# Turning the second half's tokens on VectorE and through DRAM in a fused attention and Mish MLP kernel

## The chip, the cores and the metric

The kernel runs on one core of a Trainium2 chip. The metric is the device time of one execution in microseconds; all times here are in microseconds unless another unit stands beside them. The engines are named as the profile names them: PE is TensorE's matmul, PEld its weight load, DVE is VectorE, ACT is ScalarE, POOL is GpSimd, and SP is SyncE, on which every DMA of this kernel is issued, in order.

## The reference

```python
xn = _layernorm(x)                        # x: 1 x 2048 x 576
qkv = (xn @ wqkv)                         # 32 heads of 18
# each token attends to 8 tokens: itself and those 2, 4, .. 14 before it
logits = einsum("bhsd,bhswd->bhsw", q, kg) * 18 ** -0.5
o = einsum("bhsw,bhswd->bhsd", softmax(masked logits), vg)
h = xn @ w1 + b1                          # 576 -> 4608
act = h * tanh(softplus(h))               # Mish
return x + o @ wo + act @ w2
```

Everything is fp32.

## The kernel before

**Precision and products.** Every matmul operand is held as a high and a low part: the high part is a cast (ScalarE), the low part what the cast lost (a subtraction on VectorE or GpSimd). A product is three matmuls: high by high, high by low, low by high. On top of that the MLP products are arranged as 2 x 2 block products with fewer multiplications, so that sums of blocks are formed first (names S1 to S4 on the activations' side, T1 to T4 on the weights' side) and their results are added up afterwards.

**Halves, blocks, tiles.** The 2048 tokens are worked on in two halves (`hf` 0 and 1) of 8 tiles of 128 tokens. A half has two blocks (`b` 0 and 1) of 4 tiles (`jj`, or `n` from 0 to 7 over both blocks). `XTs[hf, b]` holds the normalised tokens of a block with the features on the partitions, high and low: four groups of 128 features and a remainder of 64. For block 0 the remainder's tile has a copy in its upper half, for block 1 there is a second remainder with the difference of the two blocks (`rems`, made on GpSimd).

**How the second half's tiles come there.** `x_load(n)` loads a tile, `norm1(n)` normalises it on ScalarE and copies the remainder on GpSimd. `ln_transpose` forms the remainder of the block and calls `transpose_split`: TensorE transposes the tile in 128x128 pieces into two PSUM tiles (five pieces for block 0, six for block 1; `ta` and `tb`, or `tt` where they lie in the banks of the MLP's outputs), ScalarE casts the high part from PSUM (line 81) and VectorE subtracts for the low part (lines 82 and 87).

**The plan.** The program's order is one list of slots, `plan`. A slot has TensorE work of its own: q for one projection item (14 matmuls of 432 columns), m for one of the six parts of an MLP-up round (`m1_part`), p for a chunk or an item of the MLP-down product, z and o for others, t for one tile's transposes. `before(i, fn)` puts background work in front of slot i: loads, casts, low parts, sums, and one step of the attention, which runs beside the rest on GpSimd (products) and VectorE (sums, softmax). The slots' indices, and the offsets in the calls of `before`, are written by hand. `pend` holds the Mish work of a slot until the next one, and `soon` what is to come first in the next slot. Each engine runs its instructions in the order of this list.

**The place in the program.** The last MLP-up round of the first half is `quad(0, 17)`, from 500.89 on. Between its parts stand the down chunks of round 16, and the transposes of block 0 of the second half. Then come the last down chunks of the first half, the projections of the second half (from about 533) with block 1's transposes among them, the part called z, and the second half's MLP. In rounds q = 1 to 8 of that the down product runs in items (e, k) that pair two rounds (`p_item`): `u_sum` forms a sum of activations, `u_high` and `u_low` split it into the unit `u` that TensorE uses. The table `ds` says how many slots before its item each of these three stands. Last come the output projections o, whose operands `o_split` prepares.

Of the kernel before, what the change touches and what calls it, by code (L numbers as in the profile page):

```python
# [8 lines left out]
F32 = mybir.dt.float32  # L9
# [30 lines left out]
def block_kernel(ctx: ExitStack, tc: tile.TileContext, x, wq, wo, w1, b1, w2, mask, out):  # L40
# [23 lines left out]
    for k in range(30):  # L64
        nc.tensor.transpose(warm[:, (k % 4) * P:(k % 4 + 1) * P], ident, ident)

    def transpose_split(src, dst, col, extra=None, pair=False):
        n = next(tpn)
        if pair:
            ta, tb = (ps.tile([P, 512], F32, tag="out", bufs=4, name=f"tt{k}_{n}") for k in range(2))  # L70
        else:
            ta = ps.tile([P, 512], F32, tag="h", bufs=4, name=f"ta_{n}")
            tb = ps.tile([P, 512], F32, tag="h", bufs=4, name=f"tb_{n}")
        for k in range(KT):
            nc.tensor.transpose(ta[:, k * P:(k + 1) * P], src[:, k * P:(k + 1) * P], ident)  # L75
# [27 lines left out]
    def x_load(n):  # L103
        xn = sb.tile([P, 5 * P], F32, tag="xn", bufs=XNB, name=f"xn_1_{n}_{next(tpn)}")
        nc.sync.dma_start(xn[:, 0:D], x_tile(1, n))
        xns[1, n] = xn

# [76 lines left out]
    def ln_transpose(hf, b, jj):  # L184
        if jj == 0:
            XTs[hf, b] = sb.tile([P, 9 + b, TB], F32R, tag=f"xt{b}", bufs=1, name=f"xt_{hf}_{b}")
        xn = xns[hf, b * JB + jj]
        if (b, jj) == (0, 0):
            rems[hf] = sb.tile([P, JB, P], F32, tag="tt", bufs=2, name=f"rem_{hf}")
        rem = rems[hf][:, jj, :]  # L190
        if b == 0:
            nc.gpsimd.tensor_copy(rem, xn[:, KT * P:])
        else:
            nc.gpsimd.tensor_tensor(out=rem, in0=rem, in1=xn[:, KT * P:], op=ALU.subtract)
        transpose_split(xn, XTs[hf, b], jj * P, rem if b else None, (hf, b) == (1, 0) and jj < 3)

    def raw_load(src, width, name):
        raw = sb.tile([P, 5 * P], F32, tag="raw", bufs=4, name=f"r{name}")
# [310 lines left out]
    pend, soon = [], []  # L509

    def attention(hf):
        kqs = [load_kq(hf, k) for k in range(PU)]
# [153 lines left out]
    def prod(ph, wt, off, X, hi, lo, first, last):  # L666
        seq = [(off + k, wl, xs + k) for k in range(2) for wl, xs in ((0, hi), (0, lo), (1, hi))]
        for i, (wk, wl, xs) in enumerate(seq):
            nc.tensor.matmul(ph, wt[:, wl, wk * P:(wk + 1) * P], X[:, xs, :],  # L669
                             start=first and i == 0, stop=last and i == len(seq) - 1,  # L670
                             skip_group_check=True)

    def rest(ph, wt, off, X, xs):
        for wl in range(2):
# [365 lines left out]
    def y_store(j):  # L1040
        nc.sync.dma_start(y_d.rearrange("(p j) d -> p j d", j=TJ)[:, j, :], accs[0][j])
# [100 lines left out]
    plan = []  # L1142
    at = {}
    US = {"q": 2.75, "z": 2.5, "p": 3.15, "t": 0.6, "o": 2.6}
    PART = (3.2, 1.4, 1.4, 1.8, 1.8, 1.8)

    def add(tag, *fns, alias=None):
        at[tag] = at[alias] = len(plan)
# [5 lines left out]
    def qi(hf, g, b, jj, alias=None):  # L1154
        add(("q", hf, g, b, jj), lambda: qkv_item(hf, g, b, jj), alias=alias)
# [5 lines left out]
        add(("m", hf, q, part), lambda: m1_part(hf, q, part), alias=alias)  # L1161

    def pr_(hf, q, b, p, alias=None):
        def end():
            if hf == 0 and q == NP - 1:
                for jj in (2 * p, 2 * p + 1):
                    y_store(b * JB + jj)
        add(("p", hf, q, b, p), lambda: ((m2_cols if hf else m2_pair)(hf, q, b, p), end()), alias=alias)

    items = []  # L1170

# [51 lines left out]
            qkv_item(0, 0, 0, n)  # L1223

    def tr(b, jj):
        add(("t", 1, b, jj), lambda: ln_transpose(1, b, jj))

    CHUNKS = ((1, 0), (1, 1), (0, 0), (0, 1))

    def quad(hf, q):  # L1230
        if q == 0:
            for part, ids in ((0, (0,)), (2, (1, 2)), (1, (3, 4)), (3, (5, 6)), (5, (7, 8)), (4, (9,))):
                for p_ in {}.get(part, ()) if hf else ():
                    zi(JB - 1, p_)
                if part == 5 and hf == 0:
                    qi(hf, NQ - 1, 0, JB - 1)
                mi(hf, 0, part)
                for i in ids:
                    at["s", hf, 0, i] = len(plan) - 1
            return  # L1240
# [169 lines left out]
    for g, (e, k, s) in enumerate(items):  # L1410
        lead = items[g - 3][2] if g >= 3 else spot(1, 0, 5) + 2 * g
        before(lead + 1, lambda e=e, k=k: p_fetch(e, k))
        for qq in range(2):
            ds = {(0, 0): (-6, -5, -5), (0, 1): (-2, -1, 0), (1, 0): (0, -4, -2), (1, 1): (0, -2, -2), (2, 0): (0, -3, -2), (2, 1): (0, -3, -2), (3, 0): (-4, -3, -2), (3, 1): (-4, -2, -1), (4, 0): (0, -3, -3), (4, 1): (0, -3, -2), (5, 0): (-1, -3, -3), (5, 1): (0, -3, -2), (6, 0): (-4, -3, -1), (6, 1): (-4, -3, -2)}[k, qq]
            for d, f in zip(ds[1:], (u_high, u_low)):
                before(s + d, lambda f=f, e=e, k=k, qq=qq: f(e, k, qq))
            s2 = items[7 * e + (0 if k == 5 else k)][2] + ds[0]
            before(s2, lambda e=e, k=k, qq=qq: u_sum(e, k, qq))
# [38 lines left out]
        before(i, lambda n=n: x_load(n))  # L1457
        before(i + 5, lambda n=n: stats1(n))
    before(i + 6, var1)
    i = spot(0, NP - 2, 0)  # L1460
    for jj in range(JB):
        before(i + 2 * jj, lambda jj=jj: x_load(jj))
        before(i + 2 * jj + 6, lambda jj=jj: norm1(jj))
        before(at["t", 1, 0, jj] + 2, lambda jj=jj: x_load(JB + jj))
    for jj in range(JB):
        before(at["p", 0, NP - 1, 1, 1] + jj, lambda jj=jj: norm1(JB + jj))
# [4 lines left out]
    before(items[3][2], x_diff)  # L1471


    att = {}
    T = [0.0]
    for p_ in plan:
        T.append(T[-1] + p_[2])
# [17 lines left out]
    for n in range(steps - len(last_steps)):  # L1495
# [4 lines left out]
    early = {0: (8,), 1: (0, 2, 4, 6, 8), 2: (0, 3, 6), 3: (0, 3, 6), 4: (0, 4, 7), 5: (0, 3, 7), 6: (1, 4, 7),  # L1500
             7: (0, 4, 7), 8: (1, 4, 8), 9: (1, 3, 7)}
    for q in range(NP):
        cuts[1] += [spot(1, q, i) for i in early.get(q, (1, 3, 5, 7, 9))]
# [40 lines left out]
    for i, (fns, bg, _) in enumerate(plan):  # L1544
        first, soon[:] = soon[:], []
        held, pend[:] = pend[:], []
        for fn in first + bg + (fns + held if i == at["m", 0, 1, 0] else held + fns):
            fn()

    last = {}  # L1550
    for ins in list(nc.cur_bb.bb.instructions):
# [43 lines left out]
```

## Time and profile before

| | us |
|---|---|
| median of 3 runs | 1114.43 (1114.26 to 1114.8) |
| the profiled execution | 1114.25 |
| its span | 1112.5 |
| TensorE busy | 1101.6 |
| VectorE busy | 849.5 |
| ScalarE busy | 499.5 |
| GpSimd busy | 790.8 |

The span runs from the first instruction to the last. A row of the timeline or of the waits has the start, the length, the engine, the line, the operation, the output and its inputs, the shapes and how many instructions the row joins; in brackets stands how long the engine was idle before it, and what it then waited for. A row of the groups has the busy time, the mean of one in ns, and the idle time before.

### The profile page before, as it was taken

What the parts mean: (1) busy time and instruction counts of PE and PEld (TensorE: products, weight loads), DVE (VectorE), ACT (ScalarE), POOL (GpSimd) and SP (SyncE); (2) the same over time, 40 slices, a digit from 0 to 9 for tenths busy, and PEclk for the clock granted to TensorE, in tenths of its full rate; (3) what the DMA queues carried; (4) which work ended last, traced back from release to release, by engine and by line L of the source; (5) the groups of instructions that cost most, each with busy time, mean ns of one, the idle gap of its engine ahead of it and who ended that gap; (6) DMA issues with size and microseconds to landing.
All of it is one profiled execution on the core that took longest, in us unless ns stands there. A gap on an engine that the chain in (4) does not pass through costs nothing.

```text
span 1112.5 us, 18203 instructions
## 1 busy us (share of the span) xinstructions
PE 1101.6 (99%) x6550; PEld 1015.2 (91%) x6550; DVE 849.5 (76%) x1367; ACT 499.5 (45%) x917; POOL 790.8 (71%) x639
## 2 busy tenths in 40 slices
PE   9999999999999999999999999999999999999998
PEld 8999899999999999999999889989989999999998
DVE  6369788888889888897656577786776677777786
ACT  5544655544454544555333354433433344343353
POOL 2479777766679688785788676666688976867532
PEclk9999999999999999999999999999999999999999
DMA  6899696868777758675597898565664657776574
GB/s 202 283 312 316 225 356 214 285 233 276 258 242 264 268 208 301 249 249 204 190 323 241 245 375 307 211 196 196 220 222 170 209 195 223 244 288 219 171 232 142
DMA packets 178270, 271.60 MB, mean 244 GB/s; under 512 B 53218, under 2 KB 120068, under 8 KB 178180
## 3 DMA queue, kind: packets, MB, share of 16 engines
q1 hardware_dynamic: 178180, 270.44, 71.6%
q8 instruction: 52, 0.85, 0.3%
q14 instruction: 38, 0.31, 0.1%
HBM read 160.39 MB, written 110.00 MB: 243 GB/s over the span
## 4 chain that ended last, share of the span: by engine, by line
PE 87%; POOL 6%; DVE 3%; issue 2%; ACT 1%; DMA 0%; SPq 0%; POOLq 0%; DVEq 0%; ACTq 0%
PE h L669 28%; PE po L767 21%; PE pq L348 9%; PE po L880 9%; PE po L859 6%; PE h L675 5%; PE o L1063 5%; PE z L446 3%; POOL pv L571 2%; POOL accP L868 1%; POOL pr L533 1%; POOL act L721 1%; POOL s L620 1%; DMA acc<-in_x 0%; PE ta L75 0%
## 5 line engine op out<-in xcount | busy, mean ns | idle before, releaser
L767 PEld LDWEIGHTS po<-w,act 128*128 128x128 f32 x1728 | 236.4, 188 | 6.0 <-POOL act L721 0.4
L767 PE MATMUL po<-w,act 128*128 128x288 f32 x1728 | 240.7, 295 | 0.1
L533 POOL TENSOR_TENSOR pr<-q,kv 128x576 f32<-128x576 f32 x128 | 196.9, 1563 | 8.5 <-DMA q<-q_d 5.0
L721 POOL TENSOR_TENSOR act<-c,act 128x512 fp32r<-128x512 f32 x81 | 107.3, 1325 | 128.6 <-ACT act L720 128.6
L571 POOL TENSOR_TENSOR pv<-L,kv 128x576 f32<-128x576 f32 x128 | 177.9, 1484 | 26.1 <-DVE L L564 21.2
L771 DVE TENSOR_TENSOR acc<-po,acc 128x288 f32<-128x288 f32 x288 | 119.4, 448 | 29.9 <-PE po L767 29.0
L348 PE MATMUL pq<-wq,xt 128*128 128x432 f32 x672 | 136.5, 361 | 1.0 <-ACT xt L81 1.0
L880 PEld LDWEIGHTS po<-w,act 128*128 128x128 f32 x960 | 130.9, 188 | 4.6 <-DVE accP L883 1.8
L880 PE MATMUL po<-w,act 128*128 128x288 f32 x960 | 133.5, 295 | 1.0 <-DVE accP L883 1.0
L348 PEld LDWEIGHTS pq<-wq,xt 128*128 128x128 f32 x672 | 125.0, 188 | 8.0 <-ACT xt L81 1.8
L715 ACT ACTIVATE c<-c,b1c 128x512 f32<-128x512 f32 x81 | 58.7, 725 | 140.7 <-DVE c L714 140.4
L669 PE MATMUL h<-xt,t 128*128 128x512 f32 x432 | 110.6, 391 | 0.5 <-DVE rt L714 0.3
L669 PE MATMUL h<-S,t 128*128 128x512 f32 x432 | 110.5, 391 | 0.0
L577 DVE TENSOR_REDUCE og<-pv 128x144 f32<-128x1152 f32 x64 | 86.0, 1345 | 25.7 <-POOL pv L571 25.6
L669 PE MATMUL h<-xt,wa 128*128 128x512 f32 x432 | 104.1, 390 | 0.0
L538 DVE TENSOR_REDUCE L<-pr 128x64 f32<-128x1152 f32 x64 | 85.8, 1341 | 23.8 <-POOL pr L533 23.7
L703 ACT COPY c<-h 128x512 f32<-128x512 f32 x81 | 47.4, 586 | 124.1 <-PE h L675 73.0
L859 PEld LDWEIGHTS po<-pw,u 128*128 128x128 f32 x672 | 92.2, 188 | 5.4 <-DVE u L813 2.1
L859 PE MATMUL po<-pw,u 128*128 128x288 f32 x672 | 94.3, 295 | 2.5 <-DVE u L813 1.6
L669 PEld LDWEIGHTS h<-xt,wa 128*128 128x128 f32 x432 | 80.9, 188 | 17.0
L669 PEld LDWEIGHTS h<-xt,t 128*128 128x128 f32 x432 | 79.0, 188 | 15.7 <-DVE rt L714 0.7
L883 DVE TENSOR_TENSOR accP<-po,accP 128x288 f32<-128x288 f32 x160 | 68.9, 452 | 29.8 <-PE po L880 28.2
(228 smaller groups left out, 1853.8 us busy)
## 6 DMA issues: line engine op xcount, KB each, us to landing
kv<-kv_d SPq DMA_DIRECT2D x64, 396.0 KB, 5.1
kept_t<-t SPq DMA_DIRECT2D x36, 512.0 KB, 4.8
t<-kept_t SPq DMA_DIRECT2D x36, 512.0 KB, 6.7
rw<-in_w SPq DMA_DIRECT2D x36, 320.0 KB, 4.4
kept_wa<-wa SPq DMA_DIRECT2D x18, 640.0 KB, 4.7
kept_w<-w SPq DMA_DIRECT2D x20, 576.0 KB, 4.1
wa<-kept_wa SPq DMA_DIRECT2D x18, 640.0 KB, 5.2
w<-kept_w SPq DMA_DIRECT2D x20, 576.0 KB, 4.1
```

Of the source, the lines that this page charges most:

```text
L348: nc.tensor.matmul(pq[:, 0:432], XT[:, xi, tok], wt[wi][:, hl, 0:432], start=i == 0, stop=i == len(seq) - 1)
L533: nc.gpsimd.tensor_tensor(out=pr[:, x:x + hh], in0=q[:, j0 + x:j0 + x + hh, None, :].to_broadcast([P, hh, W, CU]), in1=win(kt, 0, CU, j0 + ...
L538: nc.vector.tensor_reduce(L[:, k, j0:j0 + hj].rearrange("p j w h -> p (j w h)"), pr.rearrange("p j w (h d) -> p (j w h) d", h=2), axis=AX, ...
L571: nc.gpsimd.tensor_tensor(out=pr[:, x:x + hj].rearrange("p j d w -> p j w d"), in0=L[:, k, x:x + hj, :, h:h + 1].to_broadcast([P, hj, W, DH]),
L577: nc.vector.tensor_reduce(og[:, c0:c0 + DH, :].rearrange("p d j -> p j d"), pr, axis=AX, op=ALU.add)
L669: nc.tensor.matmul(ph, wt[:, wl, wk * P:(wk + 1) * P], X[:, xs, :], start=first and i == 0, stop=last and i == len(seq) - 1, skip_group_ch ...
L721: nc.gpsimd.tensor_tensor(out=a[:, 1, :], in0=t, in1=a[:, 0, :].bitcast(F32), op=ALU.subtract)
L767: nc.tensor.matmul(po, acts[hf, q, b, j][:, al, tok], done["w2", hf, 2 * q + j][:, wl, c * HC:(c + 1) * HC], start=i == 0, stop=i == 5)
L771: nc.vector.tensor_tensor(out=t, in0=po, in1=t, op=ALU.add)
L859: nc.tensor.matmul(po, units[e, k, qq][:, al, tok], w[:, qq, wl, :], start=i == 0, stop=i == 5)
L880: nc.tensor.matmul(po, acts[hf, q, b, j][:, al, tok], done["w2", hf, 2 * q + j][:, wl, c * HC:(c + 1) * HC], start=i == 0, stop=i == 5)
L883: nc.vector.tensor_tensor(out=t, in0=po, in1=t, op=ALU.add)
```

## The change

1. The second half's tiles are no longer transposed on TensorE. `norm1` no longer copies the remainder. `x_turn(n)` transposes the tile in blocks of 32x32 on VectorE, into one of two buffers. `x_put(n)` writes the result to DRAM in four stores, one for each 32 partitions, in pieces of 128 bytes, so that it lies there with features as rows. `x_back(n)` loads it again with the features on the partitions, in three loads. `x_high(n)` casts on ScalarE, `x_low(n)` subtracts on VectorE, both with the loaded tile in SBUF as their source. The t slots stay in the list and have no TensorE work. The tiles of block 1 are loaded into buffers of the weights' raw tiles. The splits of a tile stand 1 to 13 slots later than its transposes stood, the loads and the normalisation earlier.
2. The stores of the first half's result (`y_store`) stand two slots later.
3. Part 1 of the second half's first MLP round is cut in two: its last three matmuls are part 6, in front of part 5.
4. `u_low` for the unit (0, 0, 1) stands one slot earlier. For the unit (3, 0, 0) the sum, the high and the low part stand one slot later.
5. The attention steps of round q = 2 of the second half stand at the places 0, 4, 7 instead of 0, 3, 6.
6. At the item (3, 4) an attention sum that was due ahead of the slot's own work is put behind it (`behind_adds`, `tail`).
7. The first `o_split` is put behind the slot's own work, with its second step one slot later.

```diff
-        if pair:
-            ta, tb = (ps.tile([P, 512], F32, tag="out", bufs=4, name=f"tt{k}_{n}") for k in range(2))
...
     def norm1(n):
         xn = xns[1, n]
         nc.scalar.activation(xn[:, 0:D], xn[:, 0:D], AF.Identity, bias=nm1[:, n, :], scale=rs1[:, n, :])
-        nc.gpsimd.tensor_copy(xn[:, D:D + 64], xn[:, KT * P:D])
+
+    def x_turn(n):
+        if n == 0:
+            xTs["a"] = sb.tile([P, D], F32, tag="acc", bufs=9, name="xT_a")
+            xTs["b"] = sb.tile([P, 2 * 432], F32, tag="r3", bufs=1, name="xT_b")[:, 0:D]
+        t = xTs["ab"[n % 2]]
+        nc.vector.transpose(t, xns[1, n][:, 0:D])
+        xTs[n] = t
+
+    def x_put(n):
+        t = xTs[n]
+        d = xT_d[n] = dram.tile([D, P], F32, name=f"xT_d{n}")
+        rows = d.rearrange("(n i) p -> i n p", i=32)
+        for g in range(4):
+            part = slice(g * 32, (g + 1) * 32)
+            nc.sync.dma_start(rows[:, :, part], t[part].rearrange("i (n k) -> i n k", k=32))
+
+    def x_back(n):
+        xn = xns[1, n] = sb.tile([P, 5 * P], F32, tag="xn", bufs=XNB, name=f"xn_t_{n}")
+        nc.sync.dma_start(xn[:, 0:KT * P].rearrange("p (k t) -> p k t", k=KT),
+                          xT_d[n][0:KT * P].rearrange("(k p) t -> p k t", p=P))
+        for r_ in range(2):
+            nc.sync.dma_start(xn[r_ * 64:(r_ + 1) * 64, KT * P:], xT_d[n][KT * P:D])
...
+    def x_high(n):
...
+        for s_, hi, lo in x_parts(n):
+            nc.scalar.copy(hi, s_)
+
+    def x_low(n):
+        for k, (s_, hi, lo) in enumerate(x_parts(n)):
+            r_ = slice(64 if k else 0, P)
+            nc.vector.tensor_tensor(out=lo[r_], in0=s_[r_], in1=hi[r_].bitcast(F32), op=ALU.subtract)
...
             if behind[0] is not None:
-                behind[0]()
+                if now[0] in behind_adds:
+                    tail.append(behind[0])
+                else:
+                    behind[0]()
...
         elif part == 1:
-            prod(bank(hf, q, 3), t1, 0, X1, 0, 5, True, True)
+            prod(bank(hf, q, 3), t1, 0, X1, 0, 5, True, True, range(3) if (hf, q) == (1, 0) else range(6))
+        elif part == 6:
+            prod(cur[3], t1, 0, X1, 0, 5, True, True, range(3, 6))
...
+            if (e, k, qq) == (0, 0, 1):
+                ds = (-2, -1, -1)
+            if (e, k, qq) == (OC - 1, 0, 0):
+                ds = (-5, -4, -4)
...
+    i, e = spot(0, NP - 3, 8), at["t", 1, 0, JB - 1]
+    for n in range(TJ):
+        b_, jj = divmod(n, JB)
+        turn = (e - 7, e - 4, e - 1, e + 2)[jj] if b_ else i + 3 * jj + 3
+        load_at = (e - 13, e - 12, e - 10, e - 6)[jj] if b_ else i + 3 * jj
+        split = e + (8, 10, 12, 13)[jj] if b_ else e + (-5, -2, 1, 4)[jj]
...
-        before(j + (1, 1, 2, 3)[k], lambda k=k: o_split(0, k, True))
+        plan[j + (1, 2, 2, 3)[k]][0].append(lambda k=k: o_split(0, k, True))
...
+        while tail:
+            tail.pop(0)()
```

How instructions move is shown at three places. The first is VectorE in the last MLP-up round of the first half, between the additions of two down chunks (`acc`). The names `m` and `L` are the softmax's, `xt_0` is `XTs[1, 0]`, `tt` a transposed tile in PSUM, and `c_0_17` the sum of two parts of an up product, whose Mish a later chunk uses. Before:

```order
L562 TENSOR_REDUCE m_5_5999<-L_5_5642 128x32
L563 RECIPROCAL m_5_5999<-m_5_5999 128x32
L564 TENSOR_TENSOR L_5_5642<-L_5_5642,m_5_5999 128x256
L82 TENSOR_TENSOR xt_0_6052<-tt_50_6129,xt_0_6052 128x4x128
L87 TENSOR_TENSOR xt_0_6052<-tt_50_6130,xt_0_6052 64x128
L714 TENSOR_TENSOR c_0_17_6008<-h_0_17_5954,c_0_17_6008 128x512
L771 TENSOR_TENSOR acc_0_2_171<-po_16_0_2_0_6157,acc_0_2_171 128x288
```

Now, with a 32x32 transpose of a later tile (`xT_b`) in front of that addition, and low parts that read the loaded tile (`xn_t`):

```order
L612 TENSOR_REDUCE m_5_6031<-L_5_5643 128x32
L613 RECIPROCAL m_5_6031<-m_5_6031 128x32
L614 TENSOR_TENSOR L_5_5643<-L_5_5643,m_5_6031 128x256
L185 TENSOR_TENSOR xt_0_6141<-xn_t_6023,xt_0_6141 128x4x128
L185 TENSOR_TENSOR xt_0_6141<-xn_t_6023,xt_0_6141 64x128
L143 STREAM_TRANSPOSE xT_b<-xn_5_49_5970 128x576
L765 TENSOR_TENSOR c_0_17_6040<-h_0_17_5977,c_0_17_6040 128x512
L824 TENSOR_TENSOR acc_0_2_171<-po_16_0_2_0_6185,acc_0_2_171 128x288
```

The low parts stand where they stood, and the transpose is one instruction more ahead of `c_0_17`.

The second place is VectorE ahead of the first item (0, 0) of the second half's down product, which TensorE runs on the units `u_0_0` and `u_0_1`. The names `rm`, `ra` and `rt` are raw activations, `og` an attention sum. Before:

```order
L577 TENSOR_REDUCE og_0_7441<-pv_0_0_0_7442 128x8x18
L801 TENSOR_TENSOR rm_7261<-rt_7264,rm_7261 128x512
L714 TENSOR_TENSOR ra_7257<-h_1_2_7499,ra_7257 128x512
L813 TENSOR_TENSOR u_0_1_7510<-rm_7262,u_0_1_7510 128x512
L801 TENSOR_TENSOR rm_7262<-rt_7265,rm_7262 128x512
L577 TENSOR_REDUCE og_0_7441<-pv_0_0_1_7483 128x8x18
L801 TENSOR_TENSOR ra_7255<-ra_7255,rm_7261 128x512
```

Now:

```order
L627 TENSOR_REDUCE og_0_7463<-pv_0_0_0_7464 128x8x18
L866 TENSOR_TENSOR u_0_1_7532<-rm_7284,u_0_1_7532 128x512
L854 TENSOR_TENSOR rm_7283<-rt_7286,rm_7283 128x512
L765 TENSOR_TENSOR ra_7279<-h_1_2_7521,ra_7279 128x512
L854 TENSOR_TENSOR rm_7284<-rt_7287,rm_7284 128x512
L854 TENSOR_TENSOR ra_7277<-ra_7277,rm_7283 128x512
L627 TENSOR_REDUCE og_0_7463<-pv_0_0_1_7505 128x8x18
```

The low part `u_0_1` has moved ahead of a sum and of an addition from PSUM (`ra<-h`), and the attention sum behind another sum.

The third place is SyncE's queue of DMAs at the end of the first half's MLP. The names `y_d` and `acc` are the result of the first half, `kv` a load for the attention, `o_d<-oT` the stores of an attention output, `wq` a projection weight. Before:

```order
L1041 DMA y_d<-acc_0_0_113 128x576
L1041 DMA y_d<-acc_0_1_117 128x576
L491 DMA kv_0_12_6401<-kv_d_129 128x792
L1041 DMA y_d<-acc_0_2_171 128x576
L1041 DMA y_d<-acc_0_3_173 128x576
L602 DMA o_d_134<-oT_5_6437 32x18x32 x4
L491 DMA kv_0_13_6461<-kv_d_129 128x792
L282 DMA wq_5_6493<-kept_wq_436 128x864
```

Now, where `xn_t` are the loads of turned tiles:

```order
L1094 DMA y_d<-acc_0_0_113 128x576
L1094 DMA y_d<-acc_0_1_117 128x576
L537 DMA kv_0_12_6439<-kv_d_129 128x792
L156 DMA xn_t_6475<-xT_d_6261 128x4x128
L159 DMA xn_t_6475<-xT_d_6261 64x128 x2
L652 DMA o_d_134<-oT_5_6473 32x18x32 x4
L156 DMA xn_t_6488<-xT_d_6366 128x4x128
L159 DMA xn_t_6488<-xT_d_6366 64x128 x2
L1094 DMA y_d<-acc_0_2_171 128x576
L1094 DMA y_d<-acc_0_3_173 128x576
L537 DMA kv_0_13_6498<-kv_d_129 128x792
L328 DMA wq_5_6520<-kept_wq_436 128x864
```

The last two tiles' loads stand around the stores of the attention output, and the stores of the result have moved behind them.

More of the change, by code (lines that the diff above doesn't have):

```diff
@@ L101, in x_tile, with x_load @@
         return x[hf * SH:(hf + 1) * SH, :].rearrange("(p j) d -> p j d", j=TJ)[:, n, :]
[L103 to L104 removed]
+    def x_load(n, tag="xn"):
+        xn = sb.tile([P, 5 * P], F32, tag=tag, bufs=BUFS[tag], name=f"xn_1_{n}_{next(tpn)}")
         nc.sync.dma_start(xn[:, 0:D], x_tile(1, n))
@@ L194, in ln_transpose @@
             nc.gpsimd.tensor_tensor(out=rem, in0=rem, in1=xn[:, KT * P:], op=ALU.subtract)
-        transpose_split(xn, XTs[hf, b], jj * P, rem if b else None, (hf, b) == (1, 0) and jj < 3)
+        transpose_split(xn, XTs[hf, b], jj * P, rem if b else None)
     def raw_load(src, width, name):
@@ L507, in win @@
                        ap=[list(base.ap[0]), [CU, jn], [DIL * CU, W], [1, cn]])
-    pend, soon = [], []
+    pend, soon, tail = [], [], []
+    behind_adds, now = set(), [0]
     def attention(hf):
@@ L664, in bank, with prod @@
         return cur[n]
-    def prod(ph, wt, off, X, hi, lo, first, last):
+    def prod(ph, wt, off, X, hi, lo, first, last, some=range(6)):
         seq = [(off + k, wl, xs + k) for k in range(2) for wl, xs in ((0, hi), (0, lo), (1, hi))]
         for i, (wk, wl, xs) in enumerate(seq):
-            nc.tensor.matmul(ph, wt[:, wl, wk * P:(wk + 1) * P], X[:, xs, :],
-                             start=first and i == 0, stop=last and i == len(seq) - 1,
-                             skip_group_check=True)
+            if i in some:
+                nc.tensor.matmul(ph, wt[:, wl, wk * P:(wk + 1) * P], X[:, xs, :],
+                                 start=first and i == 0, stop=last and i == len(seq) - 1,
+                                 skip_group_check=True)
     def rest(ph, wt, off, X, xs):
@@ L1163, in pr_ @@
     def pr_(hf, q, b, p, alias=None):
[L1164 to L1168, printed above, removed]
+        add(("p", hf, q, b, p), lambda: (m2_cols if hf else m2_pair)(hf, q, b, p), alias=alias)
     items = []
@@ L1236, in quad @@
                     qi(hf, NQ - 1, 0, JB - 1)
+                elif part == 5:
+                    mi(hf, 0, 6)
                 mi(hf, 0, part)
@@ L1459, in block_kernel @@
     before(i + 6, var1)
[L1460 to L1466, printed above, removed]
+    i, e = spot(0, NP - 3, 8), at["t", 1, 0, JB - 1]
[4 more added lines that the diff above has]
+        split = e + (8, 10, 12, 13)[jj] if b_ else e + (-5, -2, 1, 4)[jj]
+        before(load_at, lambda n=n: x_load(n, "raw" if n >= JB else "xn"))
+        before(turn - 1, lambda n=n: norm1(n))
+        before(turn, lambda n=n: x_turn(n))
+        before(turn + 2, lambda n=n: x_put(n))
+        before(e + (3, 5, 7, 8)[jj] if b_ else split - 5, lambda n=n: x_back(n))
+        before(split, lambda n=n: x_high(n))
+        before(split + 1, lambda n=n: x_low(n))
     for n, (name, pr) in enumerate((name, pr) for name in ("P4", "P5", "P2", "P3") for pr in range(2)):
@@ L1471, in block_kernel @@
     before(items[3][2], x_diff)
+    for n, (b, p) in enumerate(CHUNKS):
+        for jj in (2 * p, 2 * p + 1):
+            before(at["p", 0, NP - 1, b, p] + 2, lambda j=b * JB + jj: y_store(j))
     att = {}
+    behind_adds.add((at["p", "x", OC - 1, 4]))
     T = [0.0]
```

31 lines of the change are left out of this document (24 added, 7 removed).

## The prediction

> **What bounds the kernel now.** I read the busy times first, then the busy times of two stretches, then what TensorE (PE) waited for, then the timeline around each place that the change touches.
>
> ```profile
> PE 1101.6 (99%) x6550; PEld 1015.2 (91%) x6550; DVE 849.5 (76%) x1367; ACT 499.5 (45%) x917; POOL 790.8 (71%) x639
> 480.00:505.00 25.00, 25.00 (x152) 22.86 (x151) 24.19 (x32) 11.91 (x19) 22.03 (x19) 1.00 0.72 255
> 505.00:530.00 25.00, 25.00 (x170) 23.60 (x169) 18.05 (x37) 14.87 (x25) 12.20 (x16) 1.00 0.62 216
> ```
>
> TensorE has no gaps to speak of: the time is the sum of its instructions, at a granted clock of 1.00, plus a few waits. A change gains by taking instructions off TensorE or by removing a wait, and loses by making TensorE wait. The two stretches (columns: PE, its weight loads, VectorE, ScalarE, GpSimd, clock, DMA share, GB/s) are where the new VectorE work falls: VectorE has 0.81 us idle in the first, 6.95 in the second.
>
> **The transposes.** They leave TensorE: four tiles of five (block 0) and four of six (block 1).
>
> ```profile
> 489.06 1.53 PE L669 MATMUL h<-S,t 128*128 128x512 f32 x6
> 490.89 3.34 PE L767 MATMUL po<-w,act 128*128 128x288 f32 x24
> 518.72 0.60 PE L75 MATMUL tt<-ident,xn 128*128 128x128 f32 x4
> 521.11 3.34 PE L767 MATMUL po<-w,act 128*128 128x288 f32 x24
> 545.50 0.60 PE L75 MATMUL ta<-ident,xn 128*128 128x128 f32 x4
> 548.92 0.60 PE L75 MATMUL ta<-ident,xn 128*128 128x128 f32 x4
> 556.35 30.54 PE L348 MATMUL pq<-wq,xt 128*128 128x432 f32 x154
> ```
>
> An MLP-up part followed by a down chunk takes 490.89 − 489.06 = 1.83 without a transpose, 521.11 − 518.72 = 2.39 with one in front: 0.56 a tile, four times. In block 1 the distance from one transpose to the next is 548.92 − 545.50 = 3.42, and a projection item of 14 matmuls takes 30.54/154 × 14 = 2.78: about 0.65 a tile, four times. 4 × 0.56 + 4 × 0.65 = 4.8; with the smaller price for all eight 4.5, with the larger 5.2. **−4.8.**
>
> **The waits aimed at.**
>
> ```profile
> 633.49 1.66 PE L669 MATMUL h<-S,wc 128*128 128x512 f32 x6 [0.68 <-ACT rt L703]
> 654.88 0.82 PE L859 MATMUL po<-pw,u 128*128 128x288 f32 x5
> 657.27 2.78 PE L859 MATMUL po<-pw,u 128*128 128x288 f32 x19 [1.57 <-DVE u L813]
> 781.51 1.63 PE L669 MATMUL h<-xt,t 128*128 128x512 f32 x6 [0.29 <-DVE rt L714]
> 816.82 3.41 PE L859 MATMUL po<-pw,u 128*128 128x288 f32 x24 [0.82 <-ACT u L807]
> 1048.88 6.63 PE L880 MATMUL po<-w,act 128*128 128x288 f32 x48 [1.01 <-DVE accP L883]
> ```
>
> A bracket counts from the modelled end of the matmul before, later than the next could have started: five matmuls at 3.34/24 = 0.139 from 654.88 end at 655.58 by their pitch, and TensorE goes on at 657.27, 1.69 instead of 1.57. I add about 0.15 to each bracket.
>
> 633.49: three of part 1's matmuls, moved to stand there, give 3 × 0.26 = 0.78 of work while ScalarE reads the bank: 0.83 lost becomes about 0.1. **−0.7.**
>
> ```profile
> 653.93 1.61 DVE L801 TENSOR_TENSOR rm<-rt,rm 128x512 f32<-128x512 f32 x1
> 656.06 1.16 DVE L813 TENSOR_TENSOR u<-rm,u 128x512 fp32r<-128x512 f32 x1
> 657.96 1.30 POOL L813 TENSOR_TENSOR u<-rt,u 128x512 fp32r<-128x512 f32 x1 [1.30 <-ACT u L807]
> 661.25 3.33 PE L859 MATMUL po<-pw,u 128*128 128x288 f32 x24
> ```
>
> 657.27: the low part (656.06) now stands ahead of the sum that ended at 653.93 + 1.61. So it ends some 1.6 earlier, and the 1.7 go. But the next product (661.25) then starts at about 659.5 and needs GpSimd's low part, which ends at 659.26 here and not before a VectorE sum that now runs later. I give back 0.3. **−1.4.**
>
> 781.51: the sum of 0.68 us that the next row shows leaves the queue ahead of the addition that TensorE waits for. 0.29 + 0.15: **−0.4.**
>
> ```profile
> 780.17 0.68 DVE L801 TENSOR_TENSOR rm<-ra,rm 128x512 f32<-128x512 f32 x1
> 816.27 1.54 DVE L865 TENSOR_TENSOR accP<-po,accP 128x288 f32<-128x288 f32 x4
> 819.87 3.29 POOL L868 TENSOR_TENSOR accP<-accP,accP 128x576 f32<-128x576 f32 x2 [3.51 <-DVE accP L865]
> 828.41 1.29 POOL L822 TENSOR_TENSOR act<-rt,act 128x512 fp32r<-128x512 f32 x1
> 829.14 3.41 PE L880 MATMUL po<-w,act 128*128 128x288 f32 x24
> ```
>
> 816.82: the row names ScalarE, whose cast was done at 816.7; what TensorE awaits is a bank that VectorE's first addition at 816.27 frees, behind an attention sum of 1.34. With the sum behind the additions TensorE goes on 0.9 earlier. VectorE has the same work, though, so the last addition and GpSimd's joining (819.87) end as before, and with them GpSimd's low part: 828.41 + 1.29 = 829.70. TensorE needs that in the chunk at 829.14, after about five matmuls (829.8). Being 0.9 earlier it would wait 0.8 there. **−0.1.**
>
> ```profile
> 1047.06 0.41 DVE L914 TENSOR_TENSOR s<-ot,o 128x256 f32<-128x256 f32 x1
> 1048.38 1.54 DVE L883 TENSOR_TENSOR accP<-po,accP 128x288 f32<-128x288 f32 x4
> ```
>
> 1048.88: the first output split's VectorE work (1047.06 on) falls behind the additions that free banks. 1.01 + 0.15, less 0.15 for what remains: **−1.0.**
>
> **The new work, and what it makes late.** Each tile's VectorE transpose costs about 0.77 (the attention outputs' 128x576, next fence). It replaces nothing on VectorE; the low parts stay, but read SBUF in place of PSUM.
>
> ```profile
> 497.22 0.68 DVE L714 TENSOR_TENSOR c<-h,c 128x512 f32<-128x512 f32 x1
> 500.89 2.88 PE L669 MATMUL h<-xt,wa 128*128 128x512 f32 x12
> 501.14 0.67 ACT L715 ACTIVATE mn<-h,b1c 128x512 f32<-128x512 f32 x1
> 519.30 0.41 DVE L562 TENSOR_REDUCE m<-L 128x32 f32<-128x256 f32 x1
> 521.74 0.69 DVE L714 TENSOR_TENSOR c<-h,c 128x512 f32<-128x512 f32 x1
> 523.93 1.29 POOL L721 TENSOR_TENSOR act<-c,act 128x512 fp32r<-128x512 f32 x1 [0.40 <-ACT act L720]
> 527.15 3.02 PE L767 MATMUL po<-w,act 128*128 128x288 f32 x21
> L593 DVE STREAM_TRANSPOSE oT<-og 128x576 f32<-128x576 f32 x16 | 12.4, 773 | 0.3
> L255 DVE TENSOR_TENSOR t<-tt,t x36: 682/1292/1781, 94.5 to 495.9; 128x512 fp32r<-128x512 f32 x36
> ```
>
> Near 502: four turns, 3.1 us, fall where VectorE has 0.81 idle. The addition of 497.22 comes about 0.8 later, so ScalarE's Mish (501.14) ends at 502.6 instead of 501.81; the second product of the part that starts at 500.89 (after 6 matmuls, 502.25) needs its bank. **+0.4**; bounds 0 and 2.3 (3.1 − 0.8, nothing else hidden).
>
> Near 525: between the softmax's rows (from 519.30) and the addition of 521.74 now stand a low part and a turn, which the order shows. A low part with both inputs in SBUF takes 0.68 to 1.78 by L255's row, 1.29 in the middle; the old ones stood there too, so the addition falls about 0.9 back. GpSimd's low part (523.93 + 1.29 = 525.2) ends near 525.9 and the chunk at 527.15, now two microseconds earlier, needs it at 525.2. **+0.7**; bounds 0 and 1.4.
>
> The Trainium skill, SBUF — State Buffer, "Who interferes with whom", says that a VectorE instruction with two SBUF inputs contends with a GpSimd one that reads SBUF, and that the loser blocks for the other's whole instruction. L255's spread agrees. By it the low part may take 0.68 + 1.29, and this stall 1.4: the sum would be −6.6, the time 1107.8.
>
> The way back through DRAM:
>
> ```profile
> 546.87 2.05 SPq L602 DMA_DIRECT2D o_d<-oT  x4
> DMA to landing us min/median/max: 1.9/3.0/8.3
> xn<-in_x SPq DMA_DIRECT2D x16, 288.0 KB, 4.8
> ```
>
> The second row is that of the attention outputs' stores, which write the same 128-byte pieces as the tiles' new ones. The last tile's load stands behind the stores of 546.87 in SyncE's queue, so it is issued at about 548, lands at 553 by the 4.8 of a tile's load, and is split by 555 (a cast of 0.6, a low part of 1.3). Its projection item is the third of the run at 556.35: it began at 556.35 + 2 × 2.78 = 561.9, and begins now at 561.9 − 4.8 + 0.4 + 0.7 = 558.2. Slack some 3.1: **0**.
>
> At nothing I cost: ScalarE's extra casts (45% busy), GpSimd's fewer copies, the result's stores two slots later (read near the end only), the attention steps moved by a slot (other work of VectorE lies between), and SyncE's some 56 more issues at 0.5 us each (2.05/4) over 60 us. If SyncE gets stuck on a store that awaits a VectorE turn, weight loads behind it come late; their margin at the first item (about 532) is some 2 us.
>
> **Sum.** −4.8 − 0.7 − 1.4 − 0.4 − 0.1 − 1.0 + 0.4 + 0.7 = −7.3. From the profiled execution's 1114.25 (its span 1112.5) that is 1106.95; the median of the runs is 0.18 above, so **1107.1**. A difference within 0.2% (2.2 us) I count as the same: no more can be told from no change.
>
> **Rivals.**
> - *Nothing new is late.* The turns fit in gaps of their queue, and all five waits go wholly: the brackets' 0.68 + 1.57 + 0.29 + 0.82 + 1.01 = 4.37, and 5 × 0.15, make 5.1. 1114.4 − 4.8 − 5.1 = **1104.5**. For it: VectorE's 6.95 idle after 505. Against: the fullness of the stretch before. 0.11.
> - *VectorE pays for the turns.* In 480–505 it is full: 2.3 + 0.7 = 3.0 of stall in place of 1.1: **1109.0**. For: 24.19 of 25. Against: weight splits are part of it, and can be late. 0.18.
> - *The removed waits come back.* As at 816.82, a chain on VectorE or GpSimd that doesn't move takes each gain one item later: −4.8 + 1.1 gives **1110.7**. Against: 633.49 and 1048.88 have no such follower. 0.10.
> - *Slower: the tiles come back late.* Each item of block 1 waits for four short-piece stores, a load and a split. Beyond a landing of about 8 (4.8 + 3.1) each microsecond costs one; slower than before by 2.2 from 8 + 7.3 + 2.2 = 17.5 us; at 20 it ends at 1107.1 + 12 = **1119**. For: 128-byte pieces and a DMA share of 0.62 in 505–530. Against: such stores landed in 1.9 to 8.3 here. 0.09 for the slower side, and 0.06 for landings somewhat shorter (13 to 17.5), which eat most of the gain and leave the time within 0.2%.
>
> The Trainium skill, VectorE: DVE Perf Modes, "The three transpose paths", speaks for this last one: it calls a plain DMA copy that transposes by strides 19 times slower than the DMA's own transpose. The stores' 1.9 to 8.3 here do not bear that out for pieces of 128 bytes.
>
> That TensorE keeps the transposes is excluded: the new order has none for the second half.
>
> **How the numbers follow.** The forecast has the rest, 0.46. The low end is the first rival with the transposes at 5.2: 1104.1. The high end is the third with them at 4.5 and the stall near 525 at its bound of 1.4 in place of 0.7: 1110.7 + 0.3 + 0.7 = 1111.7. Outside lie the last rival's 0.15 and a little of each end. Faster by over 0.2%: 0.46 + 0.11 + 0.18 + 0.10 = 0.85; the same 0.06; slower 0.09.
>
> **What would show it.** Right: no f32 128x128 transposes between 515 and 555; the five brackets gone or under 0.2, but a new wait near 828 for GpSimd's low part; waits near 502 and 525 of under 1. Wrong: projection items of block 1 that wait for a split or a DMA (the slower rival); SyncE waiting for VectorE with weight loads behind it; a wait behind 661 as long as the one removed.

## The result, and the profile after

| | before | changed |
|---|---|---|
| median of 19 runs, us | 1114.63 | 1116.86 |
| lowest and highest | 1114.05, 1115.73 | 1115.78, 1119.67 |
| ratio, 95% interval | | 1.0024 [1.0017, 1.0030] |
| span of the profiled execution | 1112.5 | 1114.7 |

The change makes the kernel slower by 0.24%, where 0.66% faster had been forecast. The line of busy times, and the stretches of the stage, of the changed kernel (columns as in the prediction):

```profile
PE 1101.3 (99%) x6506; PEld 1010.8 (91%) x6506; DVE 858.7 (77%) x1379; ACT 500.6 (45%) x921; POOL 793.1 (71%) x631
480.00:505.00 25.00, 25.00 (x152) 22.85 (x151) 23.87 (x35) 11.80 (x19) 20.74 (x16) 1.00 0.92 253
505.00:530.00 25.00, 24.18 (x158) 22.40 (x157) 21.26 (x40) 15.36 (x24) 12.65 (x12) 1.00 0.98 278
530.00:556.00 26.00, 24.88 (x148) 23.46 (x147) 21.17 (x33) 7.08 (x24) 17.71 (x17) 1.00 0.91 253
556.00:585.00 29.00, 26.94 (x128) 24.95 (x127) 16.55 (x18) 9.93 (x27) 27.83 (x22) 0.94 1.07 351
```

TensorE issues 44 instructions fewer, but its busy time, in which the ends of matmuls are modelled, falls by only 0.3, and from 505 on it has waits. The DMA share, 0.62 before in the stretch from 505, is 0.98. The waits of TensorE in this stage, from the timeline:

```profile
526.51 3.70 PE L820 MATMUL po<-w,act 128*128 128x288 f32 x26 [0.82 <-POOL act L772]
534.41 1.46 PE L394 MATMUL pq<-wq,xt 128*128 128x432 f32 x6 [0.36 <-DMA wq<-kept_wq]
536.63 0.66 PE L394 MATMUL pq<-wq,xt 128*128 128x432 f32 x2 [0.76 <-DMA wq<-kept_wq]
564.74 0.85 PE L394 MATMUL pq<-wq,xt 128*128 128x432 f32 x3 [1.12 <-DMA wq<-kept_wq]
566.53 22.57 PE L394 MATMUL pq<-wq,xt 128*128 128x432 f32 x106 [0.94 <-DMA wq<-kept_wq]
598.13 1.45 PE L492 MATMUL z<-z_B,S 128*128 128x432 f32 x6 [0.77 <-DVE zqs L505]
```

The same instruction in both traces shows where time came and went (start of the same group; the last column is the step from the row above):

| group | before | changed | ahead (−) or behind (+) | step |
|---|---|---|---|---|
| down chunk (17, 1, 0), ahead of its wait | 527.15 | 525.17 | −1.99 | −1.99 |
| first projection item | 533.61 | 532.71 | −0.89 | +1.09 |
| chunk behind it | 536.36 | 537.12 | +0.76 | +1.65 |
| part z | 586.73 | 588.94 | +2.21 | +1.45 |
| z behind the sums S | 595.29 | 598.13 | +2.84 | +0.63 |
| part 5 of the first MLP round | 634.99 | 637.51 | +2.52 | −0.32 |
| the round behind item (0, 0) | 659.88 | 660.71 | +0.83 | −1.70 |
| 2 items later | 666.27 | 668.70 | +2.43 | +1.61 |
| behind item (3, 4) | 820.07 | 821.94 | +1.88 | −0.55 |
| next chunk but one | 832.39 | 835.22 | +2.83 | +0.95 |
| first output part | 1055.35 | 1057.04 | +1.69 | −1.14 |
| end | 1112.47 | 1114.74 | +2.27 | +0.58 |

Block 0's transposes bring 1.99 of the 2.2 that they were to bring. From there to the sums S of the part z the changed kernel loses 4.83, and the other edits bring little.

### The profile page after: what moved, and what is told of

Read it like the earlier page. It is cut to its first block, busy times and chain, and to the rows that moved or that the text cites. A ratio compares the mean times of both kernels' runs of the same rounds, so it can differ in the third digit from the quotient of the medians.

```text
span 1114.7 us, 18217 instructions
## 1 busy us (share of the span) xinstructions
PE 1101.3 (99%) x6506; PEld 1010.8 (91%) x6506; DVE 858.7 (77%) x1379; ACT 500.6 (45%) x921; POOL 793.1 (71%) x631
## 4 chain that ended last, share of the span: by engine, by line
PE 79%; POOL 8%; DVE 5%; issue 2%; DMA 2%; ACT 2%; SPq 0%; POOLq 0%; DVEq 0%; ACTq 0%
PE h L720 25%; PE po L820 20%; PE po L933 9%; PE pq L394 8%; PE o L1116 5%; PE h L726 5%; PE po L912 4%; PE z L492 3%; POOL pv L621 2%; POOL pr L583 1%; POOL accP L921 1%; POOL s L670 1%; POOL act L772 1%; DVE rm L854 1%; DMA accP<-in_x 1%
```

## The experiments

Each ratio is against the kernel before, run on the same chip in the same job.

**The change in two halves.** `slots` is the kernel before with parts 3 to 7 of the change; `dram` is the kernel before with parts 1 and 2.

> The kernel before with the other edits alone (parts 3 to 7 of the change), the transposes on TensorE. The steps between the two traces put them at -0.47 near 633, -1.70 + 1.61 near 660, -0.37 + 0.34 near 790, -0.82 + 0.95 near 825 and -1.14 + 0.57 near 1050: together -1.0, about 1113.5. If what came back near 660 came back only because of the late transfers, this shows about 1112 instead.

> The change's parts 1 and 2 alone (the tiles through DRAM, the stores later), all other edits undone. If the parts simply add up: 1116.9 + 1.0, about 1118, that is 3.3 slower than before.

Measured: slots 1113.77, ratio 0.9993 [0.9984, 1.0002]; dram 1117.93, ratio 1.0032 [1.0019, 1.0044]. The loss is in the way through DRAM; the two add up. In slots, without any of it, TensorE also gains 1.59 up to the round behind item (0, 0) and has lost 1.56 of it four groups later, so the late transfers are not what took that back. The rows of slots, from the timeline of VectorE, GpSimd and TensorE:

```profile
657.03 0.68 DVE L719 TENSOR_TENSOR ra<-h,ra 128x512 f32<-128x512 f32 x1
659.54 1.28 POOL L820 TENSOR_TENSOR u<-rt,u 128x512 fp32r<-128x512 f32 x1 [2.98 <-ACT u L814]
664.26 1.34 DVE L581 TENSOR_REDUCE og<-pv 128x144 f32<-128x1152 f32 x1
665.52 1.54 DVE L872 TENSOR_TENSOR accP<-po,accP 128x288 f32<-128x288 f32 x4
666.07 3.44 PE L866 MATMUL po<-pw,u 128*128 128x288 f32 x24 [0.55 <-issue]
```

The low part moved ahead pushes the addition `ra` back (before it started at 655.46), so Mish, cast and GpSimd's low part (657.96 before) come 1.6 later, and the next item loses 0.87: 0.33 before it starts, for a bank that ScalarE frees later, and 0.54 in it, for that low part. The other 0.70 goes in front of the item after that (666.07). Its bank is freed by the additions of 665.52, which before started at 664.59, ahead of the attention sum that now stands in front of them.

**Why the weights are late: order, or load?** `wq_early` puts seven weight loads earlier in SyncE's queue, `wq_act` issues them from ScalarE, `act_put` issues the tiles' stores from ScalarE. `big_pieces` and `one_put` keep SyncE's order and change the stores.

```diff
 # wq_early
-        before(i + d if k in (0, 3) else at[d], lambda k=k: fetch("wq", k))
+        before(i + d if k in (0, 3) else at[d] - 1, lambda k=k: fetch("wq", k))
-    for k in range(5):
-        before(at["q", 1, 0, 0, 3] + k, lambda k=k: fetch("wq", 5 + k))
+    for k, d in enumerate((("q", 1, 0, 0, 1), ("q", 1, 0, 0, 2), ("q", 1, 0, 0, 2), ("q", 1, 0, 0, 1), ("q", 1, 0, 0, 1))):
+        before(at[d], lambda k=k: fetch("wq", 5 + k))
...
 # big_pieces (d seen as 128 rows of 576), one_put the same in one DMA
-            nc.sync.dma_start(rows[:, :, part], t[part].rearrange("i (n k) -> i n k", k=32))
+            nc.sync.dma_start(rows[part], t[part])
 # act_put; wq_act the same in fetch, for the projection weights
-            nc.sync.dma_start(rows[:, :, part], t[part].rearrange("i (n k) -> i n k", k=32))
+            nc.scalar.dma_start(rows[:, :, part], t[part].rearrange("i (n k) -> i n k", k=32))
```

> The changed kernel with the loads of seven projection weights earlier in SyncE's queue: three by one slot, five for the next group at the first and second items instead of the fourth and later. Theory Q (the place in the queue): the waits for weights near 533 and 565 go, and with them the half-clock stretch after the second: 1.65 + 2.4 + 1.7 less, about 1111. Theory D (the DMA engines are full of 128-byte pieces, whatever the order): the loads land late all the same, not under 1115.

> The changed kernel with each of the tiles' stores writing 2304-byte pieces in place of 128-byte ones, the same number of DMAs and the same bytes (the tokens come back in a wrong arrangement). Theory D: the DMA share in 505 to 530 falls from 0.98 to about 0.7, SyncE's issues run ahead again, the waits for weights go: about 1111. Theory Q: the count of issues holds the queue, not their pieces: 1116 to 1117.

> The changed kernel with one store of 128 pieces of 2304 bytes for each tile in place of four, so 24 issues fewer on SyncE and the same bytes (the tokens come back in a wrong arrangement). Beside big_pieces (1114.2) it differs in the count of issues alone. Theory Q (SyncE's queue is full by count): about 12 us of its queue are freed, what was still late there goes: 1111 to 1112. Theory D (the engines' load): as big_pieces, 1114.

> The changed kernel with the tiles' 32 stores issued by ScalarE instead of SyncE: same pieces, same bytes, same count of DMAs, 32 issues fewer in SyncE's queue. Theory Q: weight loads and the tiles' loads run ahead again, 1111 to 1113. Theory D: the loads land late as before, 1116 to 1118.

> The changed kernel with the ten loads of projection weights issued by ScalarE at the same slots, so that they pass SyncE's queue by; all else as it is. Theory Q (they are late only because of what stands ahead of them in the queue): the waits for weights and the half-clock stretch go, 1111 to 1113. Theory D (the DMA engines are too full to bring them in time): 1115 to 1118.

| kernel | median, us | ratio and interval |
|---|---|---|
| wq_early | 1122.23 | 1.0068 [1.0056, 1.0081] |
| big_pieces | 1114.20 | 0.9997 [0.9988, 1.0006] |
| one_put | 1114.27 | 0.9993 [0.9984, 1.0002] |
| act_put | 1126.54 | 1.0099 [1.0085, 1.0113] |
| wq_act | 1119.22 | 1.0043 [1.0031, 1.0056] |

Neither theory holds as it was put. An earlier place for the weights delays what stands behind them: in wq_early the last tile is loaded 4.9 later (556.34 for 551.48), and z waits (3.1, 1.1 and 1.7). In wq_act, with the weights out of SyncE's queue, TensorE has no gap from 530 to 556, but z waits 2.3, 1.1 and 1.7; why is not shown. Long pieces with the same count of DMAs bring the ratio from 1.0024 to 0.9997, and in the profiled execution of big_pieces (the slowest of its eleven, 1116.18) no wait for weights is left; 24 DMAs fewer on top (one_put) gain nothing more, with one such wait of 0.91 near 565. So the pieces are a cause, and the next views ask how they act. The DMA views of the window 505 to 556, of before and of the changed kernel:

```profile
DMA packets 7263, 10.29 MB, mean 202 GB/s; under 512 B 2812, under 2 KB 4187, under 8 KB 7259
q1 hardware_dynamic: 7259, 10.23, 60.3%
wq<-kept_wq SPq DMA_DIRECT2D x7, 432.0 KB, 3.9
```

```profile
DMA packets 23254, 13.52 MB, mean 265 GB/s; under 512 B 14976, under 2 KB 20352, under 8 KB 23252
q1 hardware_dynamic: 23252, 13.48, 94.3%
wq<-kept_wq SPq DMA_DIRECT2D x6, 432.0 KB, 5.4
```

Three times the packets for a third more bytes; the engines are busy 94.3% instead of 60.3%, and the weights land in 5.4 instead of 3.9. But in big_pieces, whose weights come in time, the engines are still busy 87.8% in this window and the weights land in 5.2; the share in 505 to 530, which theory D had at about 0.7, is 0.92. So the landing is not what the long pieces mend.

What they mend is SyncE's own time: by its rows in this window, before it issues 32 DMAs in 15.6 of the 51 us; the changed kernel issues 73 in 46.0 (0.63 each), big_pieces 75 in 39.8 (0.53 each). In the changed kernel SyncE has next to no slack left, both by the count and by the length of an issue. Why an issue takes longer there is not shown. It is not the one wait that the traces do show: a DMA of this kernel is issued only when the one eight before it has landed. In wq_early three loads in a row were issued at 550.28, 551.30 and 552.14, and the DMAs eight before them landed at 550.22, 551.28 and 552.12. In the changed kernel such waits come to only 0.4 in this window.

With the queue full, the same two weight loads leave later, and the four stores of a tile take longer to issue, in SyncE's timeline of before, of the changed kernel and of big_pieces:

```profile
520.84 0.32 SPq L282 DMA_DIRECT2D wq<-kept_wq  x1
526.88 0.32 SPq L282 DMA_DIRECT2D wq<-kept_wq  x1
```

```profile
516.01 4.04 SPq L152 DMA_DIRECT2D xT_d<-xT_a  x4
529.12 0.38 SPq L328 DMA_DIRECT2D wq<-kept_wq  x1
531.26 0.53 SPq L328 DMA_DIRECT2D wq<-kept_wq  x1
```

```profile
515.57 2.81 SPq L152 DMA_DIRECT2D xT_d<-xT_a  x4
525.97 0.38 SPq L328 DMA_DIRECT2D wq<-kept_wq  x1
528.12 0.53 SPq L328 DMA_DIRECT2D wq<-kept_wq  x1
```

The Trainium skill, DMA: Bandwidth & Descriptors, "Specifications", gives 512 bytes as the least transfer for the full rate. The ratios of big_pieces and of the changed kernel agree as far as short pieces cost time. On ScalarE (act_put) four stores in a row held that engine 4.58 us, with copies behind them that TensorE awaits (a wait of 2.21 near 491): the cost changes its place and grows.

**Which block costs?** `b0_only` sends block 0's tiles through DRAM and transposes block 1's on TensorE (five pieces each, the remainders' difference on VectorE from PSUM); `b1_only` is the counterpart.

```diff
 # b0_only; b1_only with the blocks exchanged
-        add(("t", 1, b, jj))
+        add(("t", 1, b, jj), *((lambda: pe_turn(jj),) if b else ()))
...
```

> The changed kernel with only block 0's four tiles through DRAM; block 1's stay on TensorE, with five transposes instead of six (the blocks' difference is formed on VectorE from PSUM). Half the stores, loads and bytes go. Both theories: no wait for weights. 2.0 gained before 527 stays, the wait of 1.1 near 527 goes with the turn in front of it, 4 x 0.12 less in block 1, and 0.8 by the other edits (slots): 1114.6 - 3.3 = 1111.3. If the late loads stay, some 1113.

> The counterpart of b0_only: only block 1's four tiles go through DRAM, block 0's stay on TensorE as before (the remainder's transposed copy is taken from PSUM on ScalarE). Theory S (it is the sum of both blocks' transfers that is too much): no wait for weights, 4 x 0.65 and 0.8 of the other edits gained, 1.1 lost near 527, where the turn still stands: 1114.6 - 2.3 = 1112.3. Theory L (block 1's own way back is too late in this place, whatever block 0 does): waits for weights or splits between 533 and 575 remain: about 1116.

Measured: b0_only 1111.79, ratio 0.9970 [0.9959, 0.9982], the only version with right numbers that beats both kernels clear of noise; b1_only 1115.16, ratio 1.0005 [0.9996, 1.0014]. b0_only came out as expected, with the 2.0 kept and the wait near 527 down to 0.23 (a turn of block 1 stood in front of it):

```profile
525.62 6.38 PE L843 MATMUL po<-w,act 128*128 128x288 f32 x46 [0.23 <-POOL act L795]
```

In b1_only the weights come almost in time (one wait of 0.22), and still block 1's transposes bring nothing: it is theory L's side, by a split and by z. TensorE's two other waits, and VectorE's low parts of the four tiles in front of them, from its timeline:

```profile
561.41 5.22 PE L419 MATMUL pq<-wq,xt 128*128 128x432 f32 x24 [0.93 <-DVE xt L210]
597.28 1.45 PE L517 MATMUL z<-z_B,S 128*128 128x432 f32 x6 [1.73 <-DVE zqs L530]
548.59 1.15 DVE L210 TENSOR_TENSOR xt<-xn_t,xt 128x512 fp32r<-128x512 f32 x2
549.66 1.53 DVE L210 TENSOR_TENSOR xt<-rem,xt 64x128 fp32r<-64x128 f32 x1
551.22 2.13 DVE L210 TENSOR_TENSOR xt<-xn_t,xt 128x512 fp32r<-128x512 f32 x2
553.27 0.55 DVE L210 TENSOR_TENSOR xt<-rem,xt 64x128 fp32r<-64x128 f32 x1
555.11 2.97 DVE L210 TENSOR_TENSOR xt<-xn_t,xt 128x512 fp32r<-128x512 f32 x2
558.00 1.52 DVE L210 TENSOR_TENSOR xt<-rem,xt 64x128 fp32r<-64x128 f32 x1
559.55 3.11 DVE L210 TENSOR_TENSOR xt<-xn_t,xt 128x512 fp32r<-128x512 f32 x2
562.58 0.28 DVE L210 TENSOR_TENSOR xt<-rem,xt 64x128 fp32r<-64x128 f32 x1
```

They take 13.2 together. Before, a tile's low parts from PSUM took 0.69 and 0.43, 4.5 for four, though GpSimd worked beside them (the sum of 552.57 below and the next):

```profile
553.64 0.69 DVE L82 TENSOR_TENSOR xt<-ta,xt 128x512 fp32r<-128x512 f32 x1 [2.27 <-ACT xt L81]
554.37 0.43 DVE L87 TENSOR_TENSOR xt<-tb,xt 64x256 fp32r<-64x256 f32 x1
```

The changed kernel has the price with and without GpSimd in one trace. Of block 1's first tile the low parts fall where GpSimd is idle (4.63 ahead of 552.08, next view), of the last tile beside its sums (556.22 on):

```profile
548.76 1.00 DVE L185 TENSOR_TENSOR xt<-xn_t,xt 128x512 fp32r<-128x512 f32 x2
556.44 2.98 DVE L185 TENSOR_TENSOR xt<-xn_t,xt 128x512 fp32r<-128x512 f32 x2
```

**GpSimd's wait, or VectorE's low parts?** GpSimd forms the remainder of each returned tile, so it waits for the tile, with the attention's products and the sums S behind it. Changed kernel, then before (the bracket names a store of the same queue; the loads of the tile landed by 551.95):

```profile
552.08 0.47 POOL L178 TENSOR_TENSOR rem<-rem,xn_t 128x128 f32<-128x128 f32 x1 [4.63 <-DMA o_d<-oT]
555.74 0.52 POOL L178 TENSOR_TENSOR rem<-rem,xn_t 128x128 f32<-128x128 f32 x1
556.22 1.34 POOL L670 TENSOR_TENSOR s<-xt 128x512 f32<-128x512 f32 x1
```

```profile
552.57 1.30 POOL L620 TENSOR_TENSOR s<-xt 128x512 f32<-128x512 f32 x1
```

`no_pool` takes the remainders off GpSimd; `no_pool_wq` and `no_pool_one` do so on wq_act and one_put.

```diff
-            nc.gpsimd.tensor_tensor(out=rem, in0=rem, in1=xr, op=ALU.subtract)
+            nc.vector.tensor_tensor(out=rem, in0=rem, in1=xns[1, n][:, KT * P:], op=ALU.subtract)
...
```

> The changed kernel with the returned tiles' remainders taken off GpSimd (the copy on ScalarE, the difference on VectorE, same numbers), so that GpSimd's queue no longer waits for a tile to return. Theory G (GpSimd waits for the tiles with the attention's products and the S sums behind it, and the part z waits for those sums): GpSimd's first S sum comes at about 552 instead of 556.2, and the waits of z go; the waits for weights stay: 1116.9 - 0.6 to 1.0, and two or three less where the weights also come in time. Theory V (the tiles' low parts on VectorE hold the sums): the first sum stays at 556, 1117.

> The same on wq_act (weights loaded by ScalarE, 1119.2), whose z part lost 7.0 after 586.7 of the kernel before's scale. Theory G: that loss goes, about 1112 to 1113. Theory V: it stays, 1119.

> The same on one_put (one store of long pieces for each tile, wrong arrangement, 1114.3), where TensorE came 2.1 earlier to z than in the kernel before and lost 1.9 there. Theory G: the 1.9 stay gained, 1112.4. Theory V: 1114.3.

Measured: no_pool 1119.31, ratio 1.0037 [1.0025, 1.0050]; no_pool_wq 1118.05, ratio 1.0034 [1.0021, 1.0046]; no_pool_one 1116.05, ratio 1.0012 [1.0003, 1.0021]. GpSimd's first sum did come at 552.66, as theory G has it, and the time did not follow. GpSimd then runs beside VectorE's low parts, which grow (14.0 for block 1's four, 9.1 in the changed kernel), VectorE also has the differences to form, and TensorE waits for the splits (3.5 in two waits). The run adds work to VectorE, so it does not clear GpSimd's wait of blame. VectorE was taken out instead:

```diff
-            nc.vector.tensor_tensor(out=lo[r_], in0=s_[r_], in1=hi[r_].bitcast(F32), op=ALU.subtract)
+            if n >= JB:
+                nc.scalar.copy(lo[r_], s_[r_])
+            else:
+                nc.vector.tensor_tensor(out=lo[r_], in0=s_[r_], in1=hi[r_].bitcast(F32), op=ALU.subtract)
```

> b1_only (1115.2) with block 1's low parts written by ScalarE as a copy instead of VectorE's subtraction (so the low parts hold wrong numbers), all else as it is. Theory V (VectorE's subtractions from two SBUF sources, drawn out beside GpSimd, make the splits and then the S sums late): the projections' wait of 0.9 on a split and the wait of 1.7 in z go: about 1112.4. Theory G (GpSimd waits for the tile's return with the S sums behind it): GpSimd's first sums and the z wait stay: 1114 to 1115.

> The same on the changed kernel (1116.9). Theory V: the z wait goes and GpSimd's chain moves ahead, the waits for weights stay: 1114.5 to 1116. Theory G: 1116.9.

Measured: b1_low_act 1112.78, ratio 0.9985 [0.9976, 0.9994]; low_act 1116.96, ratio 1.0019 [1.0010, 1.0028]. In b1_low_act both waits are gone (for weights there are three of 0.2), with GpSimd's first sum where it was (553.47, in b1_only 553.63):

```profile
594.77 1.42 PE L520 MATMUL z<-z_B,S 128*128 128x432 f32 x6
```

That is theory V: 2.4 between the medians of b1_only and b1_low_act (2.2 by the ratios), by nothing but the low parts. The way from them to z is VectorE's order: its first split of a sum S starts at 563.52 before, at 567.86 in b1_only and at 564.42 in b1_low_act, and the next sum of GpSimd that waits for such a split at 565.38, 568.62 and 566.26. The run takes the low parts off VectorE wholly, so it does not say how much of the 2.4 is what they grew by.

low_act missed theory V's 1114.5 to 1116 and came out at theory G's number. Its profiled execution, the fastest of the eleven (1114.74), bears V out as to z, which no longer waits, but the weights still do (2.5 in four waits). Why the median shows no gain stays open: no run takes both causes, SyncE's full queue and VectorE's low parts, out of the changed kernel.

## Why the prediction was wrong, point by point

- **The transposes, −4.8.** The size was right where it can be seen: 1.99 for block 0's four (forecast 2.2). Block 1's 2.6 never showed. In b0_only, with one piece fewer a tile, block 1's projections gained 0.47 (−1.77 at 533.61, −2.24 at 556.35).
- **The wait near 525, +0.7.** Right in kind and near in size: 0.82 by its bracket, 1.09 by the groups' starts. In front of the addition the low part took 2.00 (0.97 before) and the turn 0.78; without that turn, in b0_only, the wait is 0.23. The wait near 502 (+0.4) did not come, and so the second rival, which had 2.3 there, was wrong in its place: VectorE paid near 525, and then for block 1's low parts.
- **The way back through DRAM, "Slack 3.1: 0".** The step that failed. It asked when a tile lands and whom TensorE's projection waits for. The last tile's load was issued at 551.48 (forecast 548), had landed at 554.95 (553), and its split ended at 559.6 (555). It left out that the low parts' price changes with their source (9.1 for block 1's four in the changed kernel, 13.2 in b1_only, 4.5 before), and that the splits of the sums S, on which z depends, stand behind them on VectorE. The row that said so, L255's 0.68 to 1.78, was quoted and used near 525, and at 1.3 for the last tile, but the four were not added up. The Trainium skill, SBUF — State Buffer, "Who interferes with whom", says that a VectorE instruction with two SBUF inputs contends with a GpSimd one that reads SBUF. The traces agree: the pair of 1.00 without GpSimd took 2.98 beside it, and from PSUM the 128x512 part kept its 0.69.
- **"At nothing I cost ... SyncE's some 56 more issues."** The step that failed first in time. The margin of the weights was given as some 2 us; two of them were issued 8.3 and 4.4 later (529.12 for 520.84, 531.26 for 526.88), and the price was 1.65 near 535. Of the next weights two were issued 2.5 and 1.2 later and landed in 8.1 and 8.9 (6.0 and 4.7 before), for the waits of 1.12 and 0.94 near 565; in big_pieces they took 7.8 and 7.9, but left 3.3 earlier, and nothing waited for them. The prediction spread the new issues over 60 us at 0.5 each and charged nothing. The runs showed a queue without slack: issues for 46.0 of 51 us in place of 15.6, at 0.63 each, and 39.8 with long pieces.
- **633.49, −0.7:** −0.47 in two groups, of which 0.15 came back. **657.27, −1.4:** −1.70, then +1.61; the give-back of 0.3 was the mis-sized term, for the addition that moved back by 1.6 feeds the next item, and an attention sum now delays the bank of the one after. **781.51, −0.4:** −0.46, then +0.34 by 796. **816.82, −0.1:** −0.82 and +0.95, as forecast by the same chain on GpSimd. **1048.88, −1.0:** −1.14, then +0.41. Together −3.6 were forecast and slots measured −0.8 (0.9993 of 1114.7, interval −1.8 to +0.2): the third rival's mechanism, with a chance of 0.10.
- **The slower rival** named the right place (items of block 1, short pieces) and the wrong mechanism: the stores and loads of tiles landed in 2.6 to 5.6 by their medians, not in 17.5. Not the tiles' own landing decided, but what their issues did to the weights behind them in SyncE's queue, and what their new source did to VectorE.

## What to carry to other kernels

When work leaves the bounding engine through memory, price its consumers again: here four tiles' subtractions cost up to three times as much from SBUF as from PSUM where GpSimd worked beside them. Ask of each queue not only how many entries are added but how long each takes to issue and whether any slack is left, and follow a late tile past its first reader. A wait that is removed by reordering one engine's queue pays only if the work pushed back has no reader soon after; try each part of a change alone (here block 0's way through DRAM, with the other edits and one piece fewer for each tile of block 1, is worth 0.3%).

## What the runs showed of the hardware that was not expected

TensorE's clock fell to half for 3.42 us after the two waits of 1.12 and 0.94, though work stood between them; the windows of the changed kernel (columns as above) show 9 matmuls where 19 fit:

```profile
566.42:569.84 3.42, 3.31 (x9) 3.06 (x10) 3.35 (x4) 0.96 (x3) 2.71 (x3) 0.50 1.05 395
570.00:573.40 3.40, 3.40 (x19) 3.26 (x18) 1.51 (x4) 1.15 (x5) 3.32 (x3) 1.00 1.13 322
```

The Trainium skill, TensorE: Matmul & The Clock Gate, "HAM oscillation — how this bites in real kernels", puts the rule as no idle gaps over some 3.4 us; here the clock fell after gaps of a third of that, close together. After single waits the traces show both: one of 1.77 in big_pieces was followed by 3.41 us at half clock, and one of 1.74 in one_put was not; in no_pool one of 1.79 was and another of 1.79 was not. So no threshold can be read from them. The loss of some 1.7 did not show in the changed kernel's time: six of its 19 runs kept a mean clock of 1.00, and they were no faster (1115.89 to 1119.35). In big_pieces it may have: the eight runs at 1.00 have a median of 1113.74, the three at 0.998 of 1115.45.
